# Gathering and turning the ragged last tile of a token list as a whole 128-row tile in a routed mixture-of-experts kernel

## The chip, the cores and the metric

The kernel runs as one program on one core of one Trainium2 chip. The metric is the device time of one execution in microseconds; a comparison uses the median of several executions. The engines are named as the profile names them: PE is the matrix engine (TensorE), PEld its loading of the stationary operand, DVE the vector engine, ACT the scalar engine, POOL GpSimd, SP the engine that issues most of the transfers.

## What is computed

A gated linear attention (4 batches, 8 heads, 768 steps, head width 40) makes 3,072 tokens of 320 values each. Each token then goes to the one of eight experts with the highest score, and the expert is a two-layer network:

```python
for e in range(E):
    mask = expert_idx == e
    h = np.maximum(x[mask] @ w1[e], 0.0)             # 320 -> 1024
    out[mask] = gate_w[mask, None] * (h @ w2[e])     # 1024 -> 320
```

`gate_w` is the softmax probability of the chosen expert. Everything is 32-bit.

## The kernel before

The attention part fills the first 125 us or so and writes the tokens to a table in device memory, `x_d`, of 3,073 rows; row 3,072 is a padding row of zeros. For every expert the kernel makes a list of row numbers with places for up to 512 tokens, as four columns of 128 partitions (`ids`). Places beyond the tokens of an expert hold the number of the padding row.

Two experts (the code's first pass, names `a` and `b`) are worked on early with capacity 512. The other six are ordered by their number of tokens, and list j gets a fixed capacity `CAPS = (448, 448, 384, 384, 320, 320)`. `TILES` (L46) cuts a list into tiles of 128 tokens, and for capacities 448 and 320 the last tile is one of 64. A list that overflowed its capacity would be handled by a slow path at the end of the program.

What happens to one list, and the names that matter here:

- `gather` (L324) calls `gather_rows` (L306): for each tile POOL issues one indirect transfer (L308) that fetches the listed rows of `x_d` into one of the four slots of the tile `xs`, 128 partitions by 4 by 384 values. The number of rows fetched is the length of the index column handed in, and `ids_v` (L1432) hands in 64 partitions for a tile of 64. The list for the next expert is gathered while the present one is computed. The first list's gather stands in `tokens` (L1555), the second's at L1578, the others' at L1598.
- `double` (L335) is an ACT copy that repeats columns 256 to 319 of each token behind themselves (columns 320 to 383). For a 64-row last tile that is a second copy, at L340.
- `x_chunk` (L342) turns one of three chunks of 128 columns of all the list's tokens, so that features lie on partitions: one PE transpose per tile (L349) into the PSUM tile `pt`, a transpose being a matrix multiplication with the identity in which the data is the stationary operand. For a 64-row tile the data is 64 rows by 128 columns and the identity is 64 by 64. ACT (L351, L354) and DVE (L352, L355) then split `pt` into a high and a low part, `xh`, `xl` and `xt`.
- `mm1` (L377) is the first layer, eight blocks of 8 matrix multiplications into `ph` (L385). `mm2` (L397) is the second layer, tile by tile of tokens: 24 matrix multiplications into `po` (L423) for a tile of 128, 16 (L410) for one of 64. A finished tile is scaled by its gates and scattered to the output by POOL (L442).

The order of the work is the order in which the program is written, with a list of deferred steps (`todo`) that are taken out at fixed places. The chunks of the next list are turned between the tiles of the second layer. For the first list (list 0) they follow tiles 0, 1 and 2 of the pass `b` (loop at L1574); for lists 1 to 5 chunk 0 follows tile 0 and chunks 1 and 2 follow tile 1, back to back (L1611). The SP queue loads the weights of the next expert (`raw`) as buffers come free.

So a 64-row tile is turned twelve times: three chunks in each of the four lists 0, 1, 4 and 5.

Of the kernel before, what the change touches and what calls it, by code (L numbers as in the profile page):

```python
# [11 lines left out]
F32 = mybir.dt.float32  # L12
# [13 lines left out]
DM = H * D  # L26
P = 128
# [16 lines left out]
NO = E - NE  # L44
CAPS = (448, 448, 384, 384, 320, 320)
TILES = [[slice(a, min(a + P, n)) for a in range(0, n, P)] for n in CAPS]  # L46
# [5 lines left out]
XW = 3 * P  # L52
# [13 lines left out]
def tile_mlstm_moe(  # L66
# [24 lines left out]
    V, G, A, T, SY = nc.vector, nc.gpsimd, nc.scalar, nc.tensor, nc.sync  # L91
# [15 lines left out]
    ident = cp.tile([P, P], F32, name="ident")  # L107
# [106 lines left out]
    pM = mctx.enter_context(tc.tile_pool(name="pM", bufs=2, space=PSUM))  # L214
# [91 lines left out]
    def gather_rows(xs, cols, rows=NT + 1):  # L306
        for a, c in enumerate(cols):
            G.indirect_dma_start(  # L308
                out=xs[0 : c.shape[0], a, 0:DM],
                out_offset=None,  # L310
                in_=x_d[0:rows],
                in_offset=bass.IndirectOffsetOnAxis(ap=c, axis=0),
                bounds_check=rows - 1,
                oob_is_err=False,
            )
        return xs
# [7 lines left out]
    def gather(cols):  # L324
        return gather_rows(lp.tile([P, NTT, XW], F32, name="xs", tag="xs"), cols)

    def x_tiles(pool, nm, w, tag=""):


        xh = pool.tile([P, 2, w], F32R, name=f"xh_{nm}", tag="xh" + tag)  # L330
        xl = pool.tile([P, 2, w], F32R, name=f"xl_{nm}", tag="xl" + tag)
        xt = pool.tile([P, w], F32R, name=f"xt_{nm}", tag="xt" + tag)
        return xh, xl, xt

    def double(xs, a, w=P):  # L335

        n = w // P
        A.copy(xs[:, a : a + n, DM:XW], xs[:, a : a + n, 2 * P : DM])
        if w % P:
            A.copy(xs[0 : w % P, n, DM:XW], xs[0 : w % P, n, 2 * P : DM])  # L340

    def x_chunk(x, xs, c, w=CAP):  # L342
        xh, xl, xt = x
        if c == 0:
            double(xs, 0, w)
        pt = pM.tile([P, 512], F32, name="pt", tag="pm")[:, 0:w]
        for a in range(0, w, P):
            r = min(P, w - a)
            T.transpose(pt[:, a : a + r], xs[0:r, a // P, c * P : (c + 1) * P], ident[0:r, 0:r])  # L349
        if c < 2:  # L350
            A.copy(xh[:, c, 0:w], pt)  # L351
            V.tensor_tensor(xl[:, c, 0:w], pt, xh[:, c, 0:w].bitcast(F32), ALU.subtract)  # L352
        else:
            A.copy(xt[:, 0:w], pt)  # L354
            V.tensor_tensor(xt[L:P, 0:w], pt[L:P], xt[L:P, 0:w].bitcast(F32), ALU.subtract)  # L355
# [14 lines left out]
    def hidden(nm):  # L370
        hh, hl = [], []
        for f in range(FC):
            hh.append(mp.tile([P, CAP], F32R, name=f"hh_{nm}_{f}", tag="hh", bufs=FC + 1))
            hl.append(mp.tile([P, CAP], F32R, name=f"hl_{nm}_{f}", tag="hl", bufs=FC + 1))
        return hh, hl

    def mm1(ws, x, xc, f, hs, hc):  # L377
        w1h, w1l, (xh, xl, xt) = ws["w1h"], ws["w1l"], x
        fs = slice(f * P, (f + 1) * P)
        ph = pH.tile([P, 512], F32, name="ph", tag="ph")[:, 0 : xc.stop - xc.start]  # L380
        ops = [(w[:, c, fs], xh[:, c, xc]) for c in range(2) for w in (w1h, w1l)]
        ops += [(w1h[:, c, fs], xl[:, c, xc]) for c in range(2)]
        ops += [(w[:, 2, fs], xt[:, xc]) for w in (w1h, w1l)]
        for i, (lt, rh) in enumerate(ops):
            T.matmul(ph, lt, rh, start=i == 0, stop=i == len(ops) - 1)  # L385
        hh, hl = hs[0][f][:, hc], hs[1][f][:, hc]
        A.activation(hh, ph, AF.Relu)  # L387
        full = (hc.stop - hc.start) // P * P
        V.scalar_tensor_tensor(  # L389
            hl[:, 0:full], ph[:, 0:full], 0.0, hh[:, 0:full].bitcast(F32), ALU.max, ALU.subtract  # L390
        )
        if hc.stop - hc.start > full:
            V.scalar_tensor_tensor(
                hs[0][f][:, hc.stop : hc.stop + L], ph[:, full:], 0.0, hh[:, full:].bitcast(F32), ALU.max, ALU.subtract
            )

    def mm2(ws, hs, ts_, gate, slots, nm):  # L397
        if ts_.stop - ts_.start == L:
            mm2_out(None, gate, slots, nm, mm2_tail(ws, hs, ts_, nm))
        else:  # L400
            mm2_out(mm2_sum(ws, hs, ts_, nm), gate, slots, nm)
# [131 lines left out]
    with ExitStack() as actx:  # L533
# [742 lines left out]
        for n in range(NS):  # L1276
# [74 lines left out]
            if last:  # L1351
                double(xs_a[:, 0], 0, HALF)
# [52 lines left out]
        ids = lc.tile([P, NO, NTT], U32, name="ids")  # L1405
# [21 lines left out]
        def do(k):  # L1427
            for _ in range(k):
                if todo:
                    todo.pop(0)()  # L1430

        ids_v = [[ids[0 : t.stop - t.start, j, a : a + 1] for a, t in enumerate(TILES[j])] for j in range(NO)]  # L1432
        ida_v = [ids_a[:, e, a : a + 1] for e in range(NE) for a in range(HT)]
        slots_b = [ids_b[:, e, a : a + 1] for e in range(NE) for a in range(HT)]
        hs = hidden("a")
# [15 lines left out]
        n, g = NS - 1, len(GROUPS) - 1  # L1451
# [3 lines left out]
        stage_store(n)  # L1455
        stage_xc(n)
        double(xs_a[:, 1], 0, HALF)
        work(2, 2)
        stage_xts(n // 2, pM, "pm")
# [69 lines left out]
    xs = gather(slots_b)  # L1529
# [6 lines left out]
    for f in g_split:  # L1536
        f()
    xp = x_tiles(mp, "p", CAP)
    xps = [lambda c=c: x_chunk(xp, xs, c) for c in range(3)]
    po2 = first_sum(2, {}, True)  # L1540
    po3 = first_sum(3, {14: xps[0], 18: xps[1], 22: xps[2]})
# [12 lines left out]

    def tokens():  # L1555
        nonlocal xs
        xs = gather(ids_v[0])

    ranks, places, lists, list_gates, beyond = arrange(mp)
    todo += ranks + places + [where] + lists + [tokens] + list_gates  # L1560
# [1 line left out]
    for e in range(NE):  # L1562
# [5 lines left out]
        if e == 0:  # L1568
            exps[2]["tiles"](wp, 1)
            todo += beyond  # L1570
    xp = x_tiles(mp, "2", CAP)
    xps = [lambda c=c: x_chunk(xp, xs, c, CAPS[0]) for c in range(3)]
    todo += [exps[2]["piece"](*p) for p in PIECES1]
    for i in range(NE * HT):  # L1574
        e, a = divmod(i, HT)
        mm2(exps[e]["ws"], hs, slice(i * P, (i + 1) * P), gtf[:, e, HT + a : HT + a + 1], slots_b[i], f"b{i}")
        if i == 1:
            xs_n = gather(ids_v[1])  # L1578
        if i == HT - 1:
            exps[2]["tiles"](w22[0], 2)  # L1580
            todo += [exps[2]["piece"](*p) for p in PIECES2]
        do(3 if i < HT else 4)
        if xps:
            xps.pop(0)()
    while todo:
        do(1)
    for e in range(NE, E):
        j = e - NE
        ws, x, w = exps[e]["ws"], xp, slice(0, CAPS[j])
        xps = []  # L1590
        if e + 1 < E:
            exp = exps[e + 1] = load_expert(e + 1, at[j + 1])
            exp["tiles"](wq if e % 2 == 0 else wp, 1)
            exp["tiles"](w22[(e + 1) % 2], 2)
            todo += [exp["load"](i) for i in range(7)]
            todo += [exp["piece"](*p) for p in PIECES1 + PIECES2]
            n = CAPS[j + 1]
            xs = gather(ids_v[j + 1]) if j else xs_n  # L1598
            xp = x_tiles(mp, e + 1, CAP)
            xps = [lambda c=c, xp=xp, xs=xs, n=n: x_chunk(xp, xs, c, n) for c in range(3)]  # L1600
            do(7)
        hs = hidden(e)
        for f in range(FC):
            mm1(ws, x, w, f, hs, w)
            do(1)
        parts = list(enumerate(TILES[j]))
        if e == E - 1:
            parts = parts[-1:] + parts[:-1]
        for i, (a, t) in enumerate(parts):
            mm2(ws, hs, t, gts[0 : t.stop - t.start, j, a : a + 1], ids_v[j][a], f"{e}_{a}")  # L1610
            for _ in range(1 + (i == 1)):  # L1611
                if xps:
                    xps.pop(0)()
            do(2)
        while todo:
            do(1)
        while xps:
            xps.pop(0)()
# [6 lines left out]
    with tc.If(over > 0):  # L1625
        with ExitStack() as octx:
# [49 lines left out]
            with tc.For_i(0, again, 1):  # L1676
                V.tensor_copy(expert, num)
                for n in range(NS):
                    j, b = divmod(n, B)
# [47 lines left out]
            with tc.For_i(0, E, 1) as k:  # L1727
# [10 lines left out]
                with tc.For_i(0, NS, 1) as t:  # L1738
# [10 lines left out]
                    pt = pv.tile([P, 512], F32, name="ovt", tag="ovt")  # L1749
                    xot = op.tile([P, 3, P], F32, name="xot")  # L1750
                    for c in range(3):
                        w = min(P, DM - c * P)
# [3 lines left out]
                    for f in range(FC):  # L1756
                        ph = pv.tile([P, 512], F32, name=f"ovh_{f}", tag="ovh")
                        for c in range(3):
                            w = min(P, DM - c * P)
# [73 lines left out]
```

## Time and profile before

| | |
|---|---|
| median of 3 executions | 343.52 us (343.35 to 344.12) |
| the profiled execution | 345.63 us |
| its span, first to last instruction | 343.8 us |
| mean granted clock of PE | 0.964 |
| PE busy | 314.5 us, 91% of the span, 4,107 multiplications |
| PEld busy | 297.6 us, 87% |
| DVE busy | 224.9 us, 65% |
| ACT busy | 164.0 us, 48% |
| POOL busy | 148.1 us, 43% |
| moved by transfers | 55.88 MB |

The profile comes from one execution. The table above is a sum over stages that differ, so the stage around the change has to be read by itself: the lists 0 to 5 are turned and multiplied between about 180 us and 337 us of the span.

### The profile page before, as it was taken

How to read it: one execution, taken by the hardware profiler on the slowest of the kernel's cores; microseconds unless marked ns; L12 is line 12 of the kernel's file. 1: busy time of each engine (PE TensorE's matmuls, PEld its weight loads, DVE VectorE, ACT ScalarE, POOL GpSimd, SP SyncE). 2: the span in 40 equal slices, each digit the busy share in tenths (PEclk: the TensorE clock that was granted, in tenths of full speed). 3: DMA queues.
4: the chain of work that ended last, by engine and by line, in shares of the span. 5: the costliest groups of instructions: out<-in, count | busy, mean ns of one | idle time of the engine just before them, and what ended most of it. 6: DMA issues, size and time to landing. Idle time of an engine off the chain costs nothing.

```text
span 343.8 us, 10433 instructions
## 1 busy us (share of the span) xinstructions
PE 314.5 (91%) x4107; PEld 297.6 (87%) x4107; DVE 224.9 (65%) x627; ACT 164.0 (48%) x433; POOL 148.1 (43%) x185
## 2 busy tenths in 40 slices
PE   6687899939998899989999999999999999999992
PEld 3687888838888789989999999999999999999992
DVE  5568469755789468988864685567566585594530
ACT  4446735524555469443345464345445464473410
POOL 6649656644668648813162710150251241232111
PEclk9599999978999899999999999999999999999997
DMA  5876668997887565102076867336348448330001
GB/s 159 286 253 203 175 202 281 267 213 264 236 259 224 146 213 154 39 5 73 22 244 232 236 214 223 116 104 204 117 122 224 125 134 232 99 97 36 14 10 45
DMA packets 26627, 55.88 MB, mean 163 GB/s; under 512 B 3487, under 2 KB 15468, under 8 KB 26570
## 3 DMA queue, kind: packets, MB, share of 16 engines
q1 hardware_dynamic: 23610, 46.55, 45.1%
q0 software_dynamic: 2560, 8.15, 7.8%
q8 instruction: 34, 0.56, 0.7%
q10 hardware_dynamic: 400, 0.43, 0.5%
q14 instruction: 23, 0.19, 0.2%
HBM read 47.29 MB, written 8.19 MB: 161 GB/s over the span
## 4 chain that ended last, share of the span: by engine, by line
PE 52%; DVE 7%; ACT 1%; issue 1%; POOL 0%; POOLq 0%; ACTq 0%; DVEq 0%
PE ph L385 24%; PE po L423 17%; PE po_b L423 4%; PE po L410 3%; PE pt L349 3%; PE po_a L423 1%; DVE hl_a L389 1%; DVE w2l L197 1%; DVE ah_all L951 0%; DVE op_all L972 0%; ACT w2h L194 0%; DVE lo L940 0%; DVE sn L470 0%; PE pg L514 0%; DVE lg_all L463 0%
## 5 line engine op out<-in xcount | busy, mean ns | idle before, releaser
L442 POOL DMA_INDIRECT out<-ob,ids x20 | 19.7, 987 | 104.4 <-DVE ob L439 85.9
L612 POOL TENSOR_TENSOR uv<-vr_s,u_t 64x328 f32<-64x328 f32 x47 | 34.9, 742 | 18.6 <-PE y L663 7.9
L423 PE MATMUL po<-w2h,hh 128*128 128x320 f32 x128 | 40.4, 316 | 0.0
L423 PE MATMUL po<-w2h,hl 128*128 128x320 f32 x128 | 39.6, 309 | 0.0
L423 PE MATMUL po<-w2l,hh 128*128 128x320 f32 x128 | 39.6, 309 | 0.0
L387 ACT ACTIVATE hh<-ph 128x448 fp32r<-128x448 f32 (+2 forms) x48 | 23.7, 493 | 33.0 <-PE ph L385 32.9
L389 DVE SCALAR_TENSOR_TENSOR hl<-ph,hh 128x384 fp32r<-128x384 f32 (+1 forms) x48 | 24.6, 513 | 15.2 <-ACT hh L387 15.0
L626 PE MATMUL s<-q_s,k_e 128*64 128x64 f32 x384 | 30.5, 238 | 3.6 <-DMA q_s<-in_qt 2.5
L701 PE MATMUL y<-uv,w_s 128*64 128x82 f32 x384 | 30.6, 247 | 3.5 <-ACT c_mid L679 3.4
L385 PE MATMUL ph<-xh,w1l 128*128 128x448 f32 (+2 forms) x96 | 32.2, 338 | 0.0
L385 PE MATMUL ph<-xh,w1h 128*128 128x448 f32 (+2 forms) x96 | 32.1, 337 | 0.0
L626 PE MATMUL s<-q_s,k_o 128*64 128x64 f32 x384 | 30.6, 238 | 1.2 <-issue 1.2
L663 PE MATMUL y<-uv,kr_s 128*40 128x41 f32 x704 | 24.4, 207 | 7.7 <-issue 5.6
L626 PEld LDWEIGHTS s<-q_s,k_e 128*64 128x64 f32 x384 | 27.4, 151 | 3.5 <-issue 1.9
L663 PEld LDWEIGHTS y<-uv,kr_s 128*40 128x40 f32 x704 | 22.4, 121 | 8.8 <-issue 6.0
L194 ACT CAST w1h<-raw 128x512 fp32r<-128x512 f32 x48 | 29.2, 617 | 0.0
L626 PEld LDWEIGHTS s<-q_s,k_o 128*64 128x64 f32 x384 | 27.4, 151 | 2.0 <-issue 2.0
L711 PE MATMUL y<-c_mid,q_s 128*64 128x82 f32 x192 | 29.0, 241 | 0.0
L439 DVE TENSOR_SCALAR ob<-po,gts 128x320 f32<-128x320 f32 x16 | 8.8, 551 | 29.8 <-PE po L423 29.8
L701 PEld LDWEIGHTS y<-uv,w_s 128*64 128x64 f32 x384 | 22.8, 143 | 6.0 <-ACT c_mid L679 4.1
L197 DVE TENSOR_TENSOR w2l<-raw,w2h 128x320 fp32r<-128x320 f32 x58 | 27.1, 505 | 0.2
L635 DVE TENSOR_TENSOR w_s<-s,late 128x512 f32<-128x512 f32 x24 | 16.6, 690 | 15.4 <-PE s L626 15.4
(332 smaller groups left out, 982.3 us busy)
## 6 DMA issues: line engine op xcount, KB each, us to landing
raw<-in_w SPq DMA_DIRECT2D x32, 320.0 KB
raw<-in_w SPq DMA_DIRECT2D x16, 512.0 KB
raw<-in_w SPq DMA_DIRECT2D x16, 256.0 KB
sig<-in_og SPq DMA_DIRECT2D x12, 320.0 KB
x_d<-x SPq DMA_DIRECT2D x12, 320.0 KB
vr_s<-in_vr SPq DMA_DIRECT2D x11, 328.0 KB
kr_s<-in_kr SPq DMA_DIRECT2D x11, 320.0 KB
q_s<-in_qt SPq DMA_DIRECT2D x22, 160.0 KB
```

What stands on the lines that cost most here:

```text
L194: A.copy(h, src)
L197: (eng or V).tensor_tensor(lo, src, h.bitcast(F32), ALU.subtract)
L385: T.matmul(ph, lt, rh, start=i == 0, stop=i == len(ops) - 1)
L387: A.activation(hh, ph, AF.Relu)
L389: V.scalar_tensor_tensor(hl[:, 0:full], ph[:, 0:full], 0.0, hh[:, 0:full].bitcast(F32), ALU.max, ALU.subtract)
L423: T.matmul(po[0 : ts_.stop - ts_.start, 0:DM], lt[f][:, ts_], rh[:, f], start=k == 0, stop=k == len(ops) - 1)
L442: store = G.indirect_dma_start(out=out, out_offset=bass.IndirectOffsetOnAxis(ap=slots, axis=0), in_=ob, in_offset=None, bounds_check=NT - ...
L612: (eng[r] if eng else G).tensor_tensor(uv[n % NB][rows, :, :, r], vr_s[q % NB][rows, k], u_t[rows, j, b].unsqueeze(3).broadcast_to([L, 2, ...
L626: T.matmul(s[r * L : r * L + L, c, a], kk[q % NB][:, k, a, cs], q_s[q % NB][:, k, a, cs], start=True, stop=True,)
L663: T.matmul(pc[r * L : r * L + D, a], kr_s[q % NB][:, k, c, a], uv[n % NB][:, c, a, r], start=n < B and c == 0 and a == 0, stop=True, skip_ ...
L701: T.matmul(ya[c], w_s[n % NB][:, c, a], uv[n % NB][:, c, a].rearrange("p r d -> p (r d)"), start=False, stop=n < B and c == 0, skip_group_ ...
L711: T.matmul(ya[c], q_s[q % NB][:, k, a, c * L : c * L + L], state[:, a], start=False, stop=True, skip_group_check=True,)
```

## The change

The last tile of a 64-row-ended list is treated as a whole tile up to the point where the first layer begins. The index columns given to `gather` are now always 128 long (`ids_g`), so that tile's transfer fetches 64 more rows, which are past the list's capacity and hold the padding row. `double` rounds the number of tiles up and needs one copy. `x_chunk` transposes 128 rows with the whole identity, and what lies past the capacity in `pt` is not read. The two layers, the scaling and the scatter still use 64.

```diff
     def double(xs, a, w=P):
-        n = w // P
+        n = -(-w // P)
         A.copy(xs[:, a : a + n, DM:XW], xs[:, a : a + n, 2 * P : DM])
-        if w % P:
-            A.copy(xs[0 : w % P, n, DM:XW], xs[0 : w % P, n, 2 * P : DM])
 
     def x_chunk(x, xs, c, w=CAP):
         xh, xl, xt = x
         if c == 0:
             double(xs, 0, w)
-        pt = pM.tile([P, 512], F32, name="pt", tag="pm")[:, 0:w]
+        pt = pM.tile([P, 512], F32, name="pt", tag="pm")
         for a in range(0, w, P):
-            r = min(P, w - a)
-            T.transpose(pt[:, a : a + r], xs[0:r, a // P, c * P : (c + 1) * P], ident[0:r, 0:r])
+            T.transpose(pt[:, a : a + P], xs[:, a // P, c * P : (c + 1) * P], ident)
+        pt = pt[:, 0:w]
...
+        ids_g = [[ids[:, j, a : a + 1] for a in range(len(TILES[j]))] for j in range(NO)]
...
-        xs = gather(ids_v[0])
+        xs = gather(ids_g[0])
...
-            xs_n = gather(ids_v[1])
+            xs_n = gather(ids_g[1])
...
-            xs = gather(ids_v[j + 1]) if j else xs_n
+            xs = gather(ids_g[j + 1]) if j else xs_n
```

No instruction changes its place. On PE, at chunk 0 of list 0, between two tiles of the pass `b`, the program before has these rows (tile written, stationary or moving operands read, then the output's shape; an "x3" stands for three alike):

```order
L423 MATMUL po_b_3429<-w2l_2533,hh_b_3119 128x320
L423 MATMUL po_b_3429<-w2h_2532,hl_b_3120 128x320
L349 MATMUL pt<-ident,xs 128x128 x3
L349 MATMUL pt<-ident,xs 128x64
L423 MATMUL po_b_3474<-w2h_2532,hh_b_3105 128x320
L423 MATMUL po_b_3474<-w2l_2533,hh_b_3105 128x320
```

and the changed program, two lines of code higher up, these:

```order
L421 MATMUL po_b_3429<-w2l_2533,hh_b_3119 128x320
L421 MATMUL po_b_3429<-w2h_2532,hl_b_3120 128x320
L346 MATMUL pt<-ident,xs 128x128 x4
L421 MATMUL po_b_3473<-w2h_2532,hh_b_3105 128x320
L421 MATMUL po_b_3473<-w2l_2533,hh_b_3105 128x320
```

The fourth transpose has become like the three before it; the same holds at the other eleven places. On ACT at the same chunk the program before has

```order
L194 CAST w1h_3317<-raw_1_3278 128x512 [waits DMAHW4_49]
L194 CAST w1h_3317<-raw_2_3280 128x512 [waits DMAHW6_49,DMAHW5_49]
L338 COPY xs<-xs 128x3x64 [waits DMASW2_49,DMASW3_49,DMASW1_49,Activation_49]
L340 COPY xs<-xs 64x64 [waits DMASW4_49]
L351 CAST xh_3426<-pt 128x448 [waits PE_49]
L194 CAST w1h_3317<-raw_0_3265 128x512
```

and the changed program

```order
L194 CAST w1h_3317<-raw_1_3278 128x512 [waits DMAHW4_49]
L194 CAST w1h_3317<-raw_2_3280 128x512 [waits DMAHW6_49,DMAHW5_49]
L338 COPY xs<-xs 128x4x64 [waits DMASW3_49,DMASW2_49,DMASW4_49,DMASW1_49,Activation_49]
L349 CAST xh_3426<-pt 128x448 [waits PE_49]
L194 CAST w1h_3317<-raw_0_3265 128x512
```

One copy now waits for all four gathers (the semaphores DMASW1 to DMASW4), where the wider of two waited for three.

## Rows read from the trace of the kernel before

**Rows 1.** Busy time of each engine from 160 to 337 us, granted clock, DMA share

```profile
core 0: us, PE busy (x) PEld busy (x) DVE busy (x) ACT busy (x) POOL busy (x), PEclk, DMA share, GB/s
160.00:337.00 177.00, 176.78 (x1168) 171.18 (x1167) 109.50 (x258) 79.71 (x184) 48.30 (x47) 1.00 0.46 137
```

**Rows 2.** Waits of PE's multiplications, 160 to 338 us: total us, times, longest

```profile
PE pg L514 <- DVE xl_p L352: 0.2, 1, 0.2
```

**Rows 3.** Waits of PE's weight loads, the same stretch: total us, times, longest

```profile
PEld pt L349 <- issue: 2.0, 12, 0.2
```

**Rows 4.** All transposes at L349: ns min/median/max, first and last start, forms

```profile
L349 PEld LDWEIGHTS pt<-ident,xs x72: 134/140/143, 160.9 to 315.9; 128*128 128x128 f32 x60, 64*128 64x128 f32 x12
L349 PE MATMUL pt<-ident,xs x72: 270/272/328, 161.0 to 315.9; 128*128 128x128 f32 x60, 64*128 64x64 f32 x12
```

**Rows 5.** Timeline of PE's weight loads, list 0, chunk 0: start us, us, what

```profile
183.67 0.39 PEld L349 LDWEIGHTS pt<-ident,xs 128*128 128x128 f32 x3
184.23 0.14 PEld L349 LDWEIGHTS pt<-ident,xs 64*128 64x128 f32 x1 [0.17 <-issue]
184.43 0.19 PEld L423 LDWEIGHTS po_b<-w2h,hh_b 128*128 128x128 f32 x1
184.54 0.19 PEld L423 LDWEIGHTS po_b<-w2l,hh_b 128*128 128x128 f32 x1
```

**Rows 6.** The same view, a chunk of pass b's tokens, four whole tiles

```profile
160.90 0.50 PEld L349 LDWEIGHTS pt<-ident,xs 128*128 128x128 f32 x4
...
161.48 0.19 PEld L423 LDWEIGHTS po_a<-w2l,hh_a 128*128 128x128 f32 x1
```

**Rows 7.** The same view, list 1, chunks 1 and 2 back to back

```profile
217.39 0.39 PEld L349 LDWEIGHTS pt<-ident,xs 128*128 128x128 f32 x3
217.95 0.51 PEld L349 LDWEIGHTS pt<-ident,xs 64*128 64x128 f32 x4 [0.17 <-issue]
...
218.94 0.19 PEld L423 LDWEIGHTS po<-w2l,hh 128*128 128x128 f32 x1
```

**Rows 8.** The same view, list 2 (384 places), chunks 1 and 2, six whole tiles

```profile
245.02 0.72 PEld L349 LDWEIGHTS pt<-ident,xs 128*128 128x128 f32 x6
...
245.82 0.19 PEld L423 LDWEIGHTS po<-w2l,hh 128*128 128x128 f32 x1
```

**Rows 9.** The same view, list 4 (320 places), chunk 0

```profile
289.00 0.29 PEld L349 LDWEIGHTS pt<-ident,xs 128*128 128x128 f32 x2
...
289.77 0.19 PEld L423 LDWEIGHTS po<-w2l,hh 128*128 128x128 f32 x1
```

**Rows 10.** The same view, list 2, chunk 0, three whole tiles

```profile
241.16 0.40 PEld L349 LDWEIGHTS pt<-ident,xs 128*128 128x128 f32 x3
...
241.64 0.19 PEld L423 LDWEIGHTS po<-w2l,hh 128*128 128x128 f32 x1
```

**Rows 11.** The same view, list 4, chunks 1 and 2

```profile
293.14 0.29 PEld L349 LDWEIGHTS pt<-ident,xs 128*128 128x128 f32 x2
...
294.48 0.19 PEld L423 LDWEIGHTS po<-w2l,hh 128*128 128x128 f32 x1
```

**Rows 12.** List 0's fourth gather (64 rows): its issue on POOL, its landing

```profile
L308 POOL DMA_INDIRECT xs<-x_d,ids x1: 956/956/956, 175.3 to 175.3; - x1
...
DMA to landing us min/median/max: 6.5/6.5/6.5
```

**Rows 13.** List 0's third gather (128 rows), the same view

```profile
L308 POOL DMA_INDIRECT xs<-x_d,ids x1: 1006/1006/1006, 174.0 to 174.0; - x1
...
DMA to landing us min/median/max: 5.9/5.9/5.9
```

**Rows 14.** List 1's four gathers (the last, of 64 rows, issued at 194.6 us)

```profile
L308 POOL DMA_INDIRECT xs<-x_d,ids x4: 946/1037/1077, 190.6 to 194.6; - x4
...
DMA to landing us min/median/max: 6.4/6.5/6.5
```

**Rows 15.** ACT: the timeline at list 0's chunk 0 (after the copies)

```profile
184.54 0.53 ACT L351 CAST xh<-pt 128x448 fp32r<-128x448 f32 x1 [1.66 <-PE pt L349]
```

**Rows 16.** ACT: all copies of a 64-row last tile at L340, ns min/median/max

```profile
L340 ACT COPY xs<-xs x4: 242/247/247, 182.6 to 308.5; 64x64 f32<-64x64 f32 x4
```

## The prediction

> **What bounds the kernel now.** I looked first at the busy time per engine over the stretch in which lists are turned and multiplied, 160 to 337 us. PE is busy for 176.78 of 177.00 us there, at a granted clock of 1.00, which is its higher level of 2.4 GHz, while ACT and DVE have half their time free [rows 1]. Next come the waits. PE's multiplications waited once, for 0.2 us, and that is before list 0 begins [rows 2]; no transfer and no other engine holds PE up from there to the last multiplication. PE's weight loads show one more kind of gap: 2.0 us in twelve pieces, all ahead of transposes at L349, with no releaser to be seen ("issue") [rows 3]. So in this stretch the end moves by what PE's own stream gets shorter or longer, and every wait that a change adds elsewhere is free as long as PE does not come to see it.
>
> Twelve gaps, and twelve 64-row transposes: the list of transposes has 72, of which 60 are whole and 12 have 64 rows [rows 4]. The timeline says where each gap sits: three whole loads in 0.39 us, 0.17 us of nothing, then the 64-row load, and the next load of the second layer only 0.20 us after that one started, at 184.43 [rows 5]. A chunk of four whole transposes shows neither the gap nor the slow return [rows 6].
>
> **What is removed on PE.** I price the whole passage rather than the gap alone: from the start of the first transpose's load to the start of the second weight load of the layer that follows, because that second one is back in step.
>
> - One chunk with a 64-row tile in a list of 448: 184.54 - 183.67 = 0.87 us [rows 5]. Four whole tiles: 161.48 - 160.90 = 0.58 us [rows 6]. Difference 0.29 us.
> - One chunk of a list of 320: 289.77 - 289.00 = 0.77 us [rows 9], against three whole tiles, 241.64 - 241.16 = 0.48 us [rows 10]. Difference 0.29 us again.
> - Two chunks back to back in a list of 448: 218.94 - 217.39 = 1.55 us, with a gap ahead of both 64-row loads, of which the row shows the first [rows 7]. Eight whole tiles don't occur. Six take 245.82 - 245.02 = 0.80 us [rows 8] and three 0.48 us [rows 10], so one more costs 0.32 / 3 = 0.107 us, and eight would take 0.80 + 0.21 = 1.01 us. Difference 0.54 us.
> - Two chunks back to back in a list of 320: 294.48 - 293.14 = 1.34 us [rows 11], against 0.80 us. Difference 0.54 us.
>
> There are six single chunks (three of list 0 and one each of lists 1, 4 and 5) and three pairs (lists 1, 4 and 5): 6 x 0.29 + 3 x 0.54 = 1.74 + 1.62 = **3.36 us**. The whole chunks are rows of the same execution, at the same clock, between the same kinds of multiplication, so this is nearly a measurement of what is left after the change. The least that can go is the idle time by itself, 2.0 us [rows 3], if the rest of the passage stayed as slow for a reason that I don't see. More than 3.36 us can't go by this path, apart from the rounding of the rows (18 ends read to 0.01 us, 0.1 us at most).
>
> Is it the size that is paid for, or the change of shape? A 64-row transpose lasts as long as a whole one: all 72 multiplications lie between 270 and 328 ns, with a median of 272 [rows 4]. So half the rows and half the columns save nothing that shows, and the price is in the change from 128 rows to 64 and back. The Trainium skill has a rule against the change: "TensorE: Matmul & The Clock Gate", section "Back-to-back issue gap", gives about 60 cycles between multiplications of up to 64 columns and 134 for 128 columns. By that, as an estimate, twelve transposes would each cost 74 cycles more, 31 ns at 2.4 GHz, and the time would rise by 0.4 us to 343.9 us. The trace does not bear this out as the price of the passage, since the narrow ones stand 0.29 us dearer.
>
> **What is added.** Four gathers fetch 64 more rows each, 64 x 1,280 B = 82 KB. Only list 0's is near its reader. Its last gather is issued at 175.3 us and lands 6.5 us later, at 181.8 [rows 12]; the fourth transpose would load at 183.67 + 0.36 = 184.03 us (four loads take 0.50 us, of which the last is 0.14) [rows 5, 6]. That is 2.2 us of cover. The price of 64 more rows lies between nothing, as the 128-row gather just before landed 5.9 us after its issue and so sooner than the one of 64 [rows 13], and a second helping of what the 64 rows added: 181.8 - 179.9 = 1.9 us between the two landings [rows 12, 13]. Even this lands at 183.7, 0.3 us ahead of PE. I take a value near the lower end, since the issue alone lasts the same (956 ns for 64 rows, 1,006 for 128), and cost it at nothing. List 1's last gather lands by 194.6 + 6.5 = 201.1 us [rows 14], and its pair of chunks is turned from 217.39 on [rows 7], its single chunk one tile of the second layer earlier; lists 4 and 5 are gathered a whole first layer ahead as well.
>
> On POOL each longer issue adds about 0.05 us, and nothing waits behind it but scatters of finished tiles. On ACT four copies of 0.24 us [rows 16] go and the other copies get 64 columns wider. The one copy now waits for the last gather too, and the conversion of `pt` is queued behind it; but ACT stood waiting 1.66 us for PE before that conversion [rows 15], and if the copy slips by all of it, PE sees it only through `pt`, of which there are two. I cost ACT and DVE at nothing. SP's queue of weight loads is unchanged.
>
> **Sum.** 345.63 - 3.36 = 342.27 us for the profiled execution. This one stands 2.11 us above the median of the runs shown; the change takes the same from both, so 343.52 - 3.36 = **340.2 us**.
>
> **Rivals.**
>
> - *List 0 lands somewhat late.* The transfers are crowded while list 0 is fetched, and a landing that comes 1 to 3 us after 184.03 takes that much back: 341.2 to 343.2 us. For it: both last gathers took 6.5 us. Against it: even twice the added time stays in front. 9%.
> - *The padding row is served one read at a time.* All 64 added rows are the same row of `x_d`. If they needed a landing of their own after the first, another 6.5 us, it would end at 188.3, PE would stand for 188.3 - 184.03 = 4.3 us at list 0, and the time would be 340.2 + 4.3 = 344.5 us. It turns slower than before once the landing passes 184.03 + 3.36 = 187.4 us, that is from 88 ns per added row. Against it: two landings 1.9 us apart in the same crowd [rows 12, 13]. 2%.
> - *The columns are paid for and the gap stays,* being tied to the last transpose of a chunk by something else. Then twelve transposes get half of 0.107 us dearer, 0.64 us, and the time is 344.2 us. Against it: the last of six whole transposes has no gap [rows 8]. 3%. The Trainium skill's rule on the issue gap, above, would come out on this side.
> - *The gain is taken back by a new wait,* since PE reaches weights and splits earlier: 343.5 us. For it: DVE is busy 109.50 of 177 us [rows 1]. Against it: ACT and DVE are paced by PE's results, and PE did not wait once for either after list 0 began [rows 2]. 4%.
>
> **How the numbers follow.** The forecast has 82%, with 339.7 to 341.0 as its own range (below: 0.17 us, by which the lowest of the three runs lies under the median, once for either set of runs, and 0.1 us of rounding; above: 0.6 us, by which the highest lies over it, and some small part of what I cost at nothing). The range reaches to 341.6 to take in the least gain of 2.0 us (341.5) and the mild half of the late landing. About 0.2%, 0.7 us, is what a measurement can tell from no change: faster is the forecast and nearly all of the late landing, 0.90; the same is the new wait and the rest of the late landing, 0.05; slower is the padding row and the columns, 0.05.
>
> **What would show it.** In the profile of the changed kernel all 72 transposes should be 128 rows by 128; the 2.0 us of "issue" ahead of L349's loads should be gone; chunk 0 of list 0 should take 0.58 us where it took 0.87, and a pair in list 1 about 1.01 where it took 1.55; list 0's last gather should land between 181.8 and 183.7 us; and the span should be near 340.4 us. It is wrong if PE waits for a DMA at about 184 us, if gaps remain ahead of the last transposes, or if a list begins its first layer with a wait for ACT or DVE.

## The result and the profile after

The changed kernel takes 339.74 us (median of 12 executions, 338.51 to 344.20) against 344.16 us for the kernel before (12 executions, 341.85 to 348.71); the ratio is 0.9892 with a 95% interval of 0.9859 to 0.9924. That is 2.6 to 4.9 us less, and the forecast was 3.36 us less. The ratio leaves out the few executions that fell into a slower state, so it lies a little nearer to 1 than that of the two medians, 0.987.

Most of the scatter is in the attention part, which the change doesn't touch: in eleven of the twelve profiles of this document the experts' first multiplication starts between 120.2 and 126.6 us, in the twelfth, which is an outlier further on as well, at 129.1. A sharper measure is the stretch that the prediction speaks of, read from one profile: from the start of the first multiplication of pass b's first layer to the end of the last one of the second layer. The chain of waits gives it, in order of time (start us, us, what). Before:

```profile
165.24 15.21 PE ph L385 x128
...
196.72 13.21 PE ph L385 x64
...
330.47 7.06 PE po L423 x48
```

After the change (the code stands two lines higher):

```profile
163.60 15.21 PE ph L383 x128
...
194.20 12.81 PE ph L383 x64
...
325.06 7.05 PE po L421 x48
```

So 337.53 - 165.24 = 172.29 us became 332.11 - 163.60 = 168.51 us: **3.78 us less**. (The chain counts the first multiplication from the end of the one before; from its own start the stretch is 172.45 and 168.68 us, and these two are what the runs below are compared with.) The profiled execution took 340.40 us, with a span of 338.5 us; of the 5.3 us between the two spans 1.6 had come before the stretch began, at 163.60 us instead of 165.24, and have nothing to do with the change.

The page after, engine by engine (busy us, share of the span, instructions):

```profile
PE 311.2 (92%) x4107; PEld 297.9 (88%) x4107; DVE 223.9 (66%) x627; ACT 162.8 (48%) x429; POOL 149.0 (44%) x185
```

As many multiplications as before, in 3.3 us less of PE's time, and four ACT instructions fewer (433 before). The stretch is as full as it was [rows 1]:

```profile
158.00:332.00 174.00, 173.78 (x1172) 171.22 (x1170) 109.87 (x258) 78.94 (x180) 49.12 (x47) 1.00 0.47 141
```

What answers to [rows 3], the waits of PE's weight loads in that stretch, no longer has a line for the transposes; one other line is left, which the kernel before has too, with the same figures, at its L514:

```profile
PEld L512 <- issue: 0.3, 1, 0.3
```

And all 72 transposes have one shape, against [rows 4]:

```profile
L346 PEld LDWEIGHTS pt<-ident,xs x72: 137/140/143, 159.2 to 310.6; 128*128 128x128 f32 x72
L346 PE MATMUL pt<-ident,xs x72: 270/272/280, 159.4 to 310.7; 128*128 128x128 f32 x72
```

The passages that the prediction priced, as the timeline of weight loads has them. List 0, chunk 0, against [rows 5]:

```profile
182.02 0.51 PEld L346 LDWEIGHTS pt<-ident,xs 128*128 128x128 f32 x4
...
182.60 0.19 PEld L421 LDWEIGHTS po_b<-w2l,hh_b 128*128 128x128 f32 x1
```

and list 1, chunks 1 and 2, against [rows 7]:

```profile
214.18 0.94 PEld L346 LDWEIGHTS pt<-ident,xs 128*128 128x128 f32 x8
...
215.20 0.19 PEld L421 LDWEIGHTS po<-w2l,hh 128*128 128x128 f32 x1
```

0.58 us where it was 0.87, and 1.02 us where it was 1.55. List 0's last gather, against [rows 12]:

```profile
L308 POOL DMA_INDIRECT xs<-x_d,ids x1: 997/997/997, 173.7 to 173.7; - x1
...
DMA to landing us min/median/max: 7.4/7.4/7.4
```

It takes 0.9 us longer to land, at 181.1 us, and the fourth transpose loads at 182.02 + 0.37 = 182.4 us. The cover of 2.2 us has shrunk to 1.3, and PE did not come to see it. That the 64 added rows are what took the 0.9 us is not shown: the third gather, of 128 rows in both kernels, takes 0.9 us longer too,

```profile
L308 POOL DMA_INDIRECT xs<-x_d,ids x1: 1003/1003/1003, 172.4 to 172.4; - x1
...
DMA to landing us min/median/max: 6.8/6.8/6.8
```

where [rows 13] have 5.9, and a run below with the old gathers lands as late.

One thing was not forecast. List 0's first layer, the same 64 multiplications over the same 448 columns, takes 13.21 us in the chain before and 12.81 us after: 0.40 us that no passage holds. The granted clock is 1.00 in both layers. The first layers of lists 1 to 5 take the same time in both kernels to within 0.02 us.

### The profile page after: what moved, and what is told of

Its sections match the earlier page's. It is cut to its first block, busy times and chain, and to the rows that moved or that the text cites. A ratio compares the mean times of both kernels' runs of the same rounds, so it can differ in the third digit from the quotient of the medians.

```text
span 338.5 us, 10430 instructions
## 1 busy us (share of the span) xinstructions
PE 311.2 (92%) x4107; PEld 297.9 (88%) x4107; DVE 223.9 (66%) x627; ACT 162.8 (48%) x429; POOL 149.0 (44%) x185
## 4 chain that ended last, share of the span: by engine, by line
PE 72%; DVE 11%; issue 5%; DMA 4%; POOL 3%; ACT 3%; SPq 1%; POOLq 0%; ACTq 0%; DVEq 0%
PE ph L383 25%; PE po L421 17%; PE s L624 5%; PE po_b L421 4%; PE y L699 4%; PE y L661 3%; PE po L408 3%; DMA q_s<-in_qt 3%; PE y L709 3%; PE pt L346 2%; POOL uv L610 2%; PE px L777 1%; PE po_a L421 1%; PE pm L797 1%; DMA raw<-in_w 1%
```

## The experiments

### The gather alone

```diff
-        n = w // P
+        n = -(-w // P)
         A.copy(xs[:, a : a + n, DM:XW], xs[:, a : a + n, 2 * P : DM])
-        if w % P:
-            A.copy(xs[0 : w % P, n, DM:XW], xs[0 : w % P, n, 2 * P : DM])
...
-        xs = gather(ids_v[0])
+        xs = gather(ids_g[0])
```

(and the other two gathers alike; the transposes as before, and the definition of `ids_g` as in the change)

> The kernel before with whole 128-row gathers and one copy in double, but the last tile still turned as 64 rows. The list stretch (from the first multiplication of pass b's first layer to the last one of the second layer) takes 172.3 us before and 168.5 us after the change. Theory (all of the price is PE's change from 128-row to 64-row transposes and back): the stretch stays at 172.3 us within 0.5, the twelve gaps of 0.17 us ahead of 64-row loads stay (2.0 us), chunk 0 of list 0 still takes 0.87 us from its first load to the second load of the layer behind it; the time is that of the kernel before. Rival (the gain comes from the single copy or the single wait for the gathers): 168.5 us. Rival (the longer gathers cost something): over 172.8 us, with a wait of PE for a DMA at about 184 us.

The stretch took 172.44 us, and the ratio to the kernel before is 1.001 (0.9977 to 1.0043, 10 executions). The waits of the weight loads are those of before:

```profile
PEld pt L347 <- issue: 2.0, 12, 0.2
```

In this stretch the longer gathers and the single copy neither give nor take anything.

### The turn alone

From the changed kernel, with the old gathers:

```diff
+        if cols[-1].shape[0] == L:
+            G.memset(xs[L:P, len(cols) - 1, 0:DM], 0.0)
...
-        xs = gather(ids_g[0])
+        xs = gather(ids_v[0])
```

(and the other two gathers alike)

> The changed kernel with the 64-row gather of the kernel before; the other 64 partitions of the last tile are set to zero by POOL ahead of the gathers of lists 0, 1, 4 and 5, so that only the turn is whole. Theory: the list stretch is that of the changed kernel, 168.5 us within 0.5 (the memsets lie on POOL, which nobody waits for); no gap ahead of a transpose. Rival (the whole gather has a part in the gain): between 168.9 and 172.3 us.

168.68 us, to the hundredth that of the changed kernel, and a ratio of 0.9901 (0.9856 to 0.9946, 10 executions). The chain has, as after the change, 332.23 - 163.72 = 168.51 us:

```profile
163.72 15.21 PE ph L386 x128
...
194.33 12.81 PE ph L386 x64
...
325.18 7.05 PE po L424 x48
```

So all of the gain is in the turn, the 0.40 us of list 0's first layer included. List 0's last gather, of 64 rows again, lands as late after its issue as the one of 128 rows in the changed kernel:

```profile
L308 POOL DMA_INDIRECT xs<-x_d,ids x1: 952/952/952, 173.5 to 173.5; - x1
...
DMA to landing us min/median/max: 7.4/7.4/7.4
```

Over the profiles that tell it, the run with added gathers aside, this landing takes 6.5, 6.6 and 7.4 us with 64 rows and 7.0 to 7.4 us with 128, so what 64 more rows cost can't be told from the scatter.

Where two kernels have the same work on PE, the stretch repeats to 0.01 us (172.45 and 172.44; 168.68 and 168.68). The experiments from here on were executed once each and are compared by this stretch.

### 64-row transposes next to each other

From the kernel before:

```diff
-        for a in range(0, w, P):
+        for a in range(0, w, P)[:: -1 if c == 2 else 1]:
```

> The kernel before with the tiles of chunk 2 turned in reverse order, so that in lists 1, 4 and 5 the 64-row transposes of chunks 1 and 2 stand next to each other: nine runs of 64-row transposes where there were twelve, but still twelve such transposes. Theory (the price is paid for each change of the height of the operand, not for each 64-row transpose): nine gaps instead of twelve, 1.5 us where there were 2.0; the pair of list 1 falls from 1.55 to about 1.28 us and those of lists 4 and 5 from 1.34 to about 1.07; the stretch is 172.3 - 0.8 = 171.5 us within 0.5. Rival (a 64-row transpose is dearer by itself): pairs unchanged, 172.3 us. In list 0, chunk 2 now begins with its 64-row transpose and should cost the same 0.87 us.

The stretch fell to 171.37 us, 1.08 less. Nine gaps are left of twelve:

```profile
PEld pt L349 <- issue: 1.5, 9, 0.2
```

and the pair of list 1 shows two 64-row loads behind one gap (the five loads of the second line are two of 64 rows and three whole ones):

```profile
217.53 0.39 PEld L349 LDWEIGHTS pt<-ident,xs 128*128 128x128 f32 x3
218.09 0.57 PEld L349 LDWEIGHTS pt<-ident,xs 64*128 64x128 f32 x5 [0.17 <-issue]
...
218.74 0.19 PEld L423 LDWEIGHTS po<-w2l,hh 128*128 128x128 f32 x1
```

1.21 us, where the two gaps of before made 1.55. The price goes with the runs, not with the transposes. The pair saves more than was expected (1.28 us), and the loads show a reason: the second narrow one starts 0.06 us behind the first, where whole ones follow each other in 0.11.

```profile
218.09 0.14 PEld L349 LDWEIGHTS pt<-ident,xs 64*128 64x128 f32 x1 [0.17 <-issue]
218.15 0.14 PEld L349 LDWEIGHTS pt<-ident,xs 64*128 64x128 f32 x1
```

So a 64-row transpose as such is about 0.05 us cheaper than a whole one (n = -0.05). In list 0, chunk 2 now begins with its narrow transpose and costs 0.25 us more than whole tiles would, not the 0.29 that was expected. What differs is what stands behind: a whole transpose here, the second layer in the other chunks. With a price d for going to 64 rows and back, four passages can be compared with those of whole tiles: a narrow one ahead of the layer costs 0.29 us, two of them with two gaps 0.53, two behind one gap 0.19, and in the next experiment a narrow one ahead of a whole one 0.24. All four come out with d = **0.34 us ahead of the second layer** and 0.29 us ahead of a whole transpose (0.34 - 0.05, 0.34 + 0.29 - 0.10, 0.29 - 0.10, 0.29 - 0.05). These prices are an estimate fitted to the passages, good to about 0.01 us.

### More changes of height

From the changed kernel, in lists 2 and 3, which had none:

```diff
         for a in range(0, w, P):
+            if w == 384 and a + P == w:
+                T.transpose(pt[:, a : a + L], xs[0:L, a // P, c * P : (c + 1) * P], ident[0:L, 0:L])
             T.transpose(pt[:, a : a + P], xs[:, a // P, c * P : (c + 1) * P], ident)
```

> The changed kernel with one more transpose of 64 rows by 64 columns ahead of the last tile's in each of the six chunks of lists 2 and 3; what it writes is overwritten by the whole transpose behind it. Theory: each brings its own 0.11 us and a change there and back of 0.27 to 0.29 us, so 6 x 0.39 = 2.3 us, and the stretch is 168.5 + 2.3 = 170.8 us within 0.5; six gaps appear. Rival (columns are what is paid for): 6 x 0.055 to 0.11 = 0.3 to 0.7 us, 168.8 to 169.2 us.

170.60 us, 1.92 more, with six gaps (1.0 us). By passages it is 0.35 us each, 2.1 us in all, of which 0.11 are the added transpose's own place in the stream and 0.24 the change there and back. The forecast of 2.3 us took no account of n, nor of the cheaper way back ahead of a whole transpose. List 2's and list 3's first layers became 0.24 us shorter at the same time, nearly all of it list 2's, after the change and here:

```profile
248.07 11.31 PE ph L383 x64
```

```profile
250.25 11.10 PE ph L385 x64
```

This is a side effect like that in list 0, but with the opposite sign: here the layer behind the breaks is the shorter one. (Pass b's first layer, ahead of the edit, is 0.06 us longer in this run, which is what one profile can be off by.)

### Which dimension: rows or columns

Instead of that transpose, a plain 16-bit multiplication, overwritten by the transpose behind it. With 64 rows:

```diff
+                T.matmul(pt[:, a : a + P], ones[0:L], iota_b[0:L], start=True, stop=True)
```

> The changed kernel with one more plain 16-bit multiplication ahead of the last tile's transpose in each of the six chunks of lists 2 and 3: 64 rows by 128 columns stationary, 128 columns moving; the transpose behind it overwrites the result. The list stretch of the changed kernel is 168.7 us. Theory (a change of the operand's height is what is paid for, whatever its width): six gaps ahead of these loads, 0.3 to 0.45 us each, stretch 170.5 to 171.4 us. Rival (it is the 64 columns of the transpose, or the transpose itself): no gap, 6 x 0.06 to 0.11 us, stretch 169.0 to 169.4 us.

and with 128 rows and 64 moving columns:

```diff
+                T.matmul(pt[:, a : a + L], ones, iota_b[:, 0:L], start=True, stop=True)
```

> The same with 128 rows by 128 columns stationary and 64 columns moving. Theory (height alone): no gap, 6 x 0.06 to 0.11 us, stretch 169.0 to 169.4 us. Rival (the width of the moving operand has a part in the price, or the change between 32-bit transposes and 16-bit multiplications has): gaps here too, stretch 170.3 us or more.

170.34 us and 168.99 us. The first lies a little below the least that was expected, 170.5, since list 2's first layer is again 0.2 us shorter (11.09 us in the chain); the second is at the lower end of its range. The timeline of weight loads at list 2's chunk 0, with 64 rows:

```profile
235.85 0.29 PEld L348 LDWEIGHTS pt<-ident,xs 128*128 128x128 f32 x2
236.30 0.09 PEld L347 LDWEIGHTS <-ones 64*128 64x128 bf16 x1 [0.17 <-issue]
236.46 0.14 PEld L348 LDWEIGHTS pt<-ident,xs 128*128 128x128 f32 x1
...
236.63 0.19 PEld L423 LDWEIGHTS po<-w2l,hh 128*128 128x128 f32 x1
```

and with 64 columns:

```profile
235.40 0.29 PEld L348 LDWEIGHTS pt<-ident,xs 128*128 128x128 f32 x2
235.66 0.10 PEld L347 LDWEIGHTS <-ones 128*128 128x128 bf16 x1
235.76 0.14 PEld L348 LDWEIGHTS pt<-ident,xs 128*128 128x128 f32 x1
...
235.94 0.19 PEld L423 LDWEIGHTS po<-w2l,hh 128*128 128x128 f32 x1
```

The passage is 0.48 us without either [rows 10]. With 64 rows it is 0.78 us and has the gap of 0.17 us; with 64 columns it is 0.54 us and has none, although the number format changes there too. It is the height of the operand, and not the transpose, its width or the format.

### How near the gather is to its reader

From the changed kernel, in `tokens`; `spare` is a tile that nobody reads:

```diff
-        xs = gather(ids_g[0])
+        xs = lp.tile([P, NTT, XW], F32, name="xs", tag="xs")
+        gather_rows(xs[:, 0:3], ids_g[0][0:3])
+        for i in range(2):
+            gather_rows(spare[:, i], ids_g[0][0:1])
+        gather_rows(xs[:, 3:4], ids_g[0][3:4])
```

> The changed kernel with two more whole gathers into a spare tile just ahead of list 0's last gather. In the changed kernel that last gather lands 1.3 us ahead of the fourth transpose. Theory (the longer gather costs nothing because of that cover, and list 0 is the one place where it could): each further gather moves the landing by 1.0 to 1.9 us, so PE waits 0.7 to 2.5 us for a DMA at list 0's chunk 0, and the stretch is 169.4 to 171.2 us. Rival (list 0's gather isn't near its reader, the transfers share the queue in another way): no wait, 168.7 us.

169.83 us, and PE waits for the gather, for the first time in this stretch:

```profile
178.31 0.40 PEld L346 LDWEIGHTS pt<-ident,xs 128*128 128x128 f32 x3
179.44 0.14 PEld L346 LDWEIGHTS pt<-ident,xs 128*128 128x128 f32 x1 [0.74 <-DMA xs<-x_d,ids]
```

Two gathers moved the landing from 1.3 us ahead of the fourth transpose to 0.74 us behind it, 1.0 us each by these two executions. So the rival of a late list 0 is a real mechanism; in the profiled execution of the changed kernel it was kept off by 1.3 us. Of the 1.15 us lost here, 0.77 us are this wait (the step from the third load to the fourth is 0.88 us and not 0.11; the loads behind it win back a few hundredths), and 0.40 us are again list 0's first layer, which is at 13.21 us in the chain.

### What sets list 0's first layer

The changed kernel with one chunk of list 0 turned as before, chunk 2 or chunk 0 (`narrow` is `(2,)` or `(0,)` for list 0 and empty elsewhere):

```diff
-            T.transpose(pt[:, a : a + P], xs[:, a // P, c * P : (c + 1) * P], ident)
+            r = min(P, w - a) if c in narrow else P
+            T.transpose(pt[:, a : a + r], xs[0:r, a // P, c * P : (c + 1) * P], ident[0:r, 0:r])
```

> The changed kernel with list 0's chunk 2 alone turned with a 64-row last tile. By its passage it costs 0.29 us. Open is why list 0's first layer takes 12.61 us after the change (first to last start) where it took 13.01. If the way into it decides (the last turn before it), it is 13.01 here and the stretch is 168.7 + 0.29 + 0.40 = 169.4 us; if the whole of the change or another chunk decides, it stays at 12.61 and the stretch is 169.0 us.

> The changed kernel with list 0's chunk 0 alone turned with a 64-row last tile, two tiles of the second layer further from list 0's first layer than in the run with chunk 2. If the cadence of list 0's first layer depends on what stands right before it, it stays at 12.61 us and the stretch is 168.7 + 0.29 = 169.0 us; if any break in PE's stream since pass b sets it, as the wait for the gather seemed to do, it is 13.01 and the stretch 169.4 us.

> The same kernel as narrow_c0 once more, since in that run PE stood 3.3 us inside pass b, before the chunk in question, behind a wait that none of the other profiles has. As before: if the cadence of list 0's first layer depends on what stands right before it, that layer takes 12.61 us from first to last start and the stretch is 168.7 + 0.29 = 169.0 us; if any break in PE's stream since pass b sets it, 13.01 and 169.4 us.

With chunk 2: 13.01 us from first to last start, stretch 169.40 us. The first run with chunk 0 decides nothing, since its stretch holds that stop of 3.3 us, after which the granted clock was at its lower level of 1.2 GHz (0.51) from 183.0 to 186.4 us (174.49 us; the layer, with a short stop of its own, at 13.10). The second run: 13.01 us and 169.44 us, and in its chain

```profile
190.45 13.21 PE ph L384 x64
```

A single change of height 11 us ahead of the layer is enough. Over the runs but that first one, the layer takes 12.60 or 12.61 us where PE's stream is unbroken from pass b to list 0 (the changed kernel, the turn alone and the three with additions in lists 2 and 3) and 13.01 us where it is broken once or more in list 0's chunks (the kernel before, the gather alone, the adjacent order, the late gather, chunk 2 and chunk 0). The granted clock is 1.00 in the layer in all of them, so the clock doesn't make the difference. The groups by shape show how, before and after (count, busy us, mean ns of one, in a window over the layer):

```profile
L385 PE MATMUL ph<-xh,w1h 128*128 128x448 f32 x16 | 5.9, 369 | 0.0
```

```profile
L383 PE MATMUL ph<-xh,w1h 128*128 128x448 f32 x16 | 5.8, 362 | 0.0
```

These multiplications run 7 ns longer, and those of the layer follow each other at an even pace of 13.01 / 63 = 0.2065 us instead of 12.61 / 63 = 0.2002 us. What locks PE to one pace or the other isn't settled by these runs; that for list 0 the way in decides it is shown, since each of the breaks did it and no run without one had it. It is no general rule: lists 1, 4 and 5 lost their breaks in the change as well, and their first layers kept their times (12.98 and 12.97, 9.38 and 9.38, 9.39 and 9.39 us in the chain), and list 2's got shorter behind added ones.

## Why the prediction was right

- *PE's own stream sets the end.* It does: a stretch that PE fills [rows 1] got shorter by what PE's passages lost and what its pace gained, and nothing else showed up at a list's start.
- *0.29 us for a single chunk, 0.54 for a pair, 3.36 us in all.* The passages after are 0.58 and 1.02 us, as the whole chunks of before said. The sum missed the whole by 3.78 - 3.36 = 0.42 us. The step that was too small is that of what is removed on PE: "more than 3.36 us can't go by this path" is wrong, because multiplications further on can run at another pace after a break in the stream, as list 0's first layer did (0.40 us). No row ahead of the change shows it, and why it happens is open.
- *The time itself.* 339.74 us lies in the range, but only just above its lower end of 339.7, and that it does is partly luck. The prediction took its base from three executions, 343.52 us; over twelve it is 344.16, and 3.36 us less would be 340.8. The span was to be near 340.4 us and was 338.5, 1.6 us of it by the attention part. What bears the prediction out is the stretch, 3.78 us shorter, and the passages.
- *The price is in the change from 128 rows to 64 and back.* Shown from three sides: adding changes of height adds it, gathering 64-row transposes into one run saves it, and a 64-column operand doesn't have it. That the narrow transposes "save nothing that shows" was too simple: it was read from the 272 ns that a transpose of either kind lasts, and the steps between them show about 0.05 us less each, which the 0.34 us for the change hid.
- *The rival by columns.* The Trainium skill's rule in "TensorE: Matmul & The Clock Gate", section "Back-to-back issue gap", by which 64 columns are cheaper than 128, agrees with the runs in its direction: a step of 0.06 us between narrow transposes where whole ones take 0.107. Its sizes, about 60 cycles and 134, would be 0.025 and 0.056 us at 2.4 GHz and are not those of this stream. But the price that decided is another. The Trainium skill's "TensorEngine Tiling (Array Packing)", section "Key Properties", says that changing the tiling mode drains the engine. The gap of 0.17 us before and the slow return behind look like that, though no run shows that a 64-row operand changes such a mode. Here the way there and back is worth 0.34 us ahead of the second layer.
- *The gathers cost nothing.* Right for PE: the gather alone changed nothing. The landing came 0.9 us later after its issue, inside the forecast's 0 to 1.9 but not at the lower end that it took, and the turn alone has the same landing with 64 rows. How much of the 0.9 us is the rows stays open; other profiles had the same gather of 64 rows 6.5 and 6.6 us after its issue.
- *The single copy, POOL, the new wait.* Nothing, as costed; the runs with the gather alone and the turn alone separate them.

## What to carry to other kernels

Where PE is the bound, as here, don't trim an operand from 128 rows to the 64 that are filled: a 64-row multiplication among whole ones cost more than a whole one that computes on padding, because PE stops on the way in and is slow on the way back. Where narrow ones are needed, put them next to each other. The price at the place itself can be read ahead of the change if the same program has the whole form somewhere, by comparing passages from the first load to the point where the stream is back in step. What a break does to the pace further on (0.40 us here) can't be read so.

## What the runs showed that I had not expected

- Going from 128 to 64 *columns* of the stationary operand and back costs nothing that shows. In the second layer's short form eight such loads stand in a row behind seven whole ones and ahead of one, and the chain before has

```profile
222.62 2.34 PE po L410 x16
...
237.95 3.52 PE po L423 x24
```

that is 0.146 us for each of 16, and 0.147 us for each of 24 that are all whole. The Trainium skill's rule on tiling modes, as cited above, does not tell the two cases apart, and here only the height had a price.

- The same multiplications of list 0 can hold one of two even paces for 13 us (0.2002 or 0.2065 us for 448 columns), and a stop 11 us earlier chooses. List 1's first layer, with 448 columns too, takes 0.203 us on average in both kernels (12.98 and 12.97 us in the chain), in steps that go up and down between 199 and 207 ns.
